# Two of four token groups turned by crossbar DMAs in the first phase of a gated attention and ReGLU training step

## The chip, the cores and the metric

The kernel runs on one core of one Trainium2 chip. The metric is the device time of one execution in microseconds (us); lower is better. The kernel before takes 909.8 us, the median of three runs (909.38 to 910.1).

## The reference

The program computes the output of a mixed layer and all its gradients for one sequence of 2048 tokens with 512 features, in bf16. For each token a gate g is the sigmoid of the product of x with a vector gate_w. One branch is a sliding-window attention with 32 heads of 16 features and a window of 256 tokens; the other is a feed-forward block with a ReLU gate and 1376 hidden columns. The part that matters for this change is the feed-forward block:

```
gate = x @ W_gate;  up = x @ W_up            # [2048,512] x [512,1376]
h    = relu(gate) * up
b    = h @ W_down
out  = g * attention(x) + (1 - g) * b
```

From grad_out the kernel also returns the gradients of x, wqkv, wo, W_gate, W_up, W_down and gate_w: eight outputs in all. For the feed-forward block, db = (1 - g) * grad_out, dh = db @ W_down^T, dg = dh * up where gate > 0, du = dh * relu(gate), and the weight gradients are x^T @ dg, x^T @ du and h^T @ db.

## The kernel before, in words

The program has three phases. The first, which the change is in, is the feed-forward block with its gradients (about the first quarter of the time). The second is the attention, forward and backward, and the third the output projections.

In the first phase the tokens lie in four groups of 512 (tg 0 to 3, TGW wide, each of four tiles of 128 tokens), and the hidden columns in 11 pieces of 128 (fc). One step is one piece for one group: 44 steps, the groups running fastest, so that steps 0 to 3 are fc 0 with the four groups, steps 4 to 7 are fc 1, and so on. The loop (L448) runs over n and does, in this order, for different steps at once:

- `gate` and `up` of step n (L365, L371): two products on TensorE (PE) of four matmuls each, from `x_T[tg]`, which holds the group's x with the features on the partitions. ScalarE (ACT) takes the ReLU into `rg`, VectorE (DVE) makes `upm`, and GpSimd (POOL) makes `hT`.
- `dh` of step n-2 (L379): a product of the turned W_down piece `WdT` with `db_T`, db with the features on the partitions; ACT copies it, DVE and POOL make dg and du, the two halves of the tile `dgu`.
- `turn_h` of step n-1 (L389) and `turn_dgu` of step n-4 (L393): crossbar DMAs on the queue of SyncE (SP), which turn `hT` and `dgu` into rows, `h_r` and `dgu_r`.
- `keep` (L398): plain DMAs on ACT's queue that store hT of step n-3 and dg and du of step n-4 to HBM.
- `weights` of step n-6 (L402): 20 matmuls on PE that add to the weight gradients, from the rows of x (`x_r`), `dgu_r`, `h_r` and the rows of db (`db_r`). So the first weights product, that of step 0, is in n = 6.

In the first steps there is more to do, once per group. `turn_x` (L292) turns a group's rows of x with 16 PE transposes of 128x128 into PSUM and two copies, one by DVE and one by ACT, into `x_T`; the x of group n+1 is turned in n. `gate_col` (L301) makes g of group n. `db_rows` (L312) scales the rows of grad_out into `db_r`: tiles 1 and 3 of the group on ACT, tile 0 on DVE, tile 2 on POOL (on DVE for the last group). `turn_db` (L321) turns them, again by 16 PE transposes and two copies, in step n+1 for group n.

The order of work is written out by hand: each engine runs its instructions in the order of the program. All loads and all crossbar DMAs stand on SP's queue, in the order of the program too. Ahead of the loop (L243 to L274) SP issues x of group 0, the first 128 columns of W_gate and W_up, x of group 1, grad_out of group 0, a piece of W_down, then x of group 2, grad_out of group 1, x of group 3, grad_out of group 2, columns 128 to 383 of both weights, grad_out of group 3, and last columns 384 to 1375 of both weights (992 KB each, `load_wgu(3 * P, F)`, L274). In the loop the queue takes `turn_h`, `turn_wd` (L227, W_down's next piece, at the first group of each fc), `turn_dgu` and, from n = 8, other turns and stores.

The tiles `dgu` have 6 buffers, `hT` 7; PSUM has 3 buffers for the products of the steps.

Of the kernel before, what the change touches and what calls it, by code (L numbers as in the profile page):

```python
# [22 lines left out]
def kernel(  # L23
# [20 lines left out]
    nc = tc.nc  # L44
    P = 128
    x_d = A_x[0]
# [4 lines left out]
    F = B_W_gate.shape[1]  # L51
# [7 lines left out]
    TGW = min(512, S)  # L59
    NTG = S // TGW  # L60
    TPG = TGW // P
# [5 lines left out]
    def evac(out, in_, eng=None):  # L67
        if eng is None:
            eng = ("act", "dve")[rr["i"] % 2]
            rr["i"] += 1  # L70
        if eng == "act":
            nc.scalar.copy(out, in_)  # L72
        elif eng == "dve":
            nc.vector.tensor_copy(out, in_)  # L74
        else:
            nc.gpsimd.tensor_copy(out, in_)
# [6 lines left out]
    dgT_d = dram.tile([F, S], BF, name="dgT_d")  # L83
    duT_d = dram.tile([F, S], BF, name="duT_d")
# [13 lines left out]
    def slot(tag):  # L98
        return big.tile([P, DC, TGW], BF, tag=tag, name=tag)

    x_T = [slot(f"x{tg}") for tg in range(NTG)]
# [96 lines left out]
    with ExitStack() as p1, tc.manual_schedule():  # L198
# [3 lines left out]
        db_r = ap1.tile([P, NT, D], BF, name="db_r")  # L202
        db_T = ap1.tile([P, DC, S], BF, name="db_T")
# [8 lines left out]
        def rows_of(ap, tg):  # L212
            return ap[tg * TGW:(tg + 1) * TGW, :].rearrange("(t p) d -> p t d", p=P)
# [6 lines left out]
        def load_go(tg):  # L220
            flat = zt[tg // 2][:].rearrange("p w k h q -> p (w k h q)")
            go_in[tg] = flat[:, (tg % 2) * TPG * D:(tg % 2 + 1) * TPG * D].rearrange("p (t d) -> p t d", t=TPG)
            nc.sync.dma_start(go_in[tg], rows_of(go_d, tg))
# [3 lines left out]
        def turn_wd(fc):  # L227
            WdT[fc] = fp.tile([P, DC, P], BF, tag="WdT", bufs=2, name="WdT")
            nc.sync.dma_start_transpose(out=WdT[fc][:], in_=B_W_down[start_of(fc):start_of(fc) + P, :])
# [3 lines left out]
        def turn_wd0():  # L233
            WdT[0] = fp.tile([P, DC, P], BF, tag="WdT", bufs=2, name="WdT")
            pt = ps1.tile([P, DC, 2, P], BF, tag="mm", bufs=3, name="ptw")
            for c in range(DC):
                nc.tensor.transpose(pt[:, c, 0, :], wd0[:, c * P:(c + 1) * P], ident[:])
            nc.vector.tensor_copy(WdT[0][:], pt[:, :, 0, :])
# [17 lines left out]
        def load_x(tg):  # L256
            nc.sync.dma_start(x_r[:, tg * TPG:(tg + 1) * TPG, :], rows_of(x_d, tg))

        def load_wgu(a, b):
            nc.sync.dma_start(Wg_sb[:, :, a:b], Wg_v[:, :, a:b])  # L260
            nc.sync.dma_start(Wu_sb[:, :, a:b], Wu_v[:, :, a:b])
# [3 lines left out]
        nc.sync.dma_start(Wu_sb[:, :, 0:W0], Wu_v[:, :, 0:W0])  # L265
        load_go(0)
        nc.sync.dma_start(wd0[:], B_W_down[0:P, :])
        load_x(2)
        load_go(1)
        load_x(3)  # L270
        load_go(2)
        load_wgu(W0, 3 * P)
        load_go(3)
        load_wgu(3 * P, F)  # L274
        nc.gpsimd.memset(par4[:], 1.0)
        nc.gpsimd.affine_select(out=par4[:], in_=par4[:], compare_op=ALU.is_ge, fill=0.0, base=0,
                                pattern=[[-32, P // 32]], channel_multiplier=1)
# [14 lines left out]
        def turn_x(tg):  # L292
            for half in range(2):
                t0 = tg * TPG + 2 * half
                pt = ps1.tile([P, DC, 2, P], BF, tag="tr", bufs=2, name="ptx")
                for c in range(DC):
                    for tt in range(2):
                        nc.tensor.transpose(pt[:, c, tt, :], x_r[:, t0 + tt, c * P:(c + 1) * P], ident[:])
                evac(x_T[tg][:, :, 2 * half * P:(2 * half + 2) * P], pt[:].rearrange("p c t q -> p c (t q)"), ("dve", "act")[half])

        def gate_col(tg):  # L301
            zps = ps1.tile([P, TPG], F32, tag="mm", bufs=3, name="zps")
            for k in range(TPG):
                t = tg * TPG + k
                for c in range(DC):
                    nc.tensor.matmul(zps[:, k:k + 1], lhsT=x_T[tg][:, c, k * P:(k + 1) * P], rhs=gw_col[:, c:c + 1],
                                     start=(c == 0), stop=(c == DC - 1))
            tsl = slice(tg * TPG, (tg + 1) * TPG)
            nc.scalar.activation(g_all[:, tsl], zps[:], ACT.Sigmoid)
            nc.vector.tensor_scalar(omg_all[:, tsl], g_all[:, tsl], -1.0, 1.0, op0=ALU.mult, op1=ALU.add)  # L310

        def db_rows(tg):  # L312
            for k in range(TPG):
                t = tg * TPG + k
                if k % 2:
                    nc.scalar.mul(db_r[:, t, :], go_in[tg][:, k, :], omg_all[:, t:t + 1])
                else:
                    eng = nc.gpsimd if k == 2 and tg < NTG - 1 else nc.vector
                    eng.tensor_scalar(db_r[:, t, :], go_in[tg][:, k, :], omg_all[:, t:t + 1], None, op0=ALU.mult)
# [45 lines left out]
        def gate(k):  # L365
            k.gps = ps1.tile([P, TGW], F32, tag="mm", bufs=3, name="gps")
            product(k.gps, lambda c: Wg_sb[:, c, k.fsl], lambda c: x_T[k.tg][:, c, :])
            k.rg = tile1("rg")
            nc.scalar.activation(k.rg[:], k.gps[:], ACT.Relu)  # L369
# [19 lines left out]
        def turn_h(k):  # L389
            k.h_r = fp.tile([P, TPG, P], BF, tag="h_r", bufs=6, name="h_r")  # L390
            nc.sync.dma_start_transpose(out=k.h_r[:], in_=k.hT[:])
# [6 lines left out]
        def keep(k, *pairs):  # L398
            for dst, src in pairs:
                nc.scalar.dma_start(dst[k.fsl, k.ts], src)  # L400
# [37 lines left out]
        def turn_gw():  # L438
            pt = ps1.tile([P, P], BF, tag="mm", bufs=3, name="ptg")
            nc.tensor.transpose(pt[:], gw_r[:], ident[:])  # L440
            nc.vector.tensor_copy(gw_col[:], pt[:, 0:DC])
# [6 lines left out]
        for n in range(N1 + 8):  # L448
            at = lambda lag: steps[n - lag] if 0 <= n - lag < N1 else None
            if at(0):  # L450
                gate(at(0))
                if 0 < n < NTG:
                    gate_col(n)
                if n == 2:
                    turn_wd0()
                if n + 1 < NTG:
                    turn_x(n + 1)
                if n == 0:
                    turn_gw()
                up(at(0))  # L460
                if n == 0:
                    gate_col(n)
                if n < NTG:
                    db_rows(n)
                if at(0).tg == 0 and at(0).fc > 0:
                    turn_wd(at(0).fc)
            if 1 <= n <= NTG:
                turn_db(n - 1)
            if at(2):
                dh(at(2))  # L470
            if at(1):
                turn_h(at(1))
            if at(3):
                keep(at(3), (hT_d, at(3).hT[:]))
            if at(4):
                turn_dgu(at(4))
                keep(at(4), (dgT_d, at(4).dgT), (duT_d, at(4).duT))
            if at(6):
                f = weights(at(6))
                if f is not None:  # L480
                    stores[n + 1] = f
            if n in stores:
                stores.pop(n)()
            t = n - DA0
            if t % 2 == 1 and 0 <= t // 2 < NT:
                make_da(t // 2)
            if t % 2 == 0 and 0 < t // 2 <= NT:
                turn_da(t // 2 - 1)
            if t == 2:
                nc.vector.reduce_sum(par[:, 0:1], par4[:], axis=AX.X)  # L490
                nc.vector.tensor_scalar(par[:, 1:2], par[:, 0:1], -1.0, 1.0, op0=ALU.mult, op1=ALU.add)
            if n == NTG + 1:
                nc.scalar.activation(tiny[:], tiny[:], ACT.Exp)
            if t in (NT + 3, 2 * NT + 1):
                i = (t - NT - 3) // (NT - 2)
                nc.gpsimd.memset(zt[i][:, 0, :, :, :], 0.0)
                nc.vector.memset(zt[i][:, 1, :, :, :], 0.0)
            if n == N1 - 2:
                first = project_parts(*groups[0])
            for _ in range({N1 + 1: 2, N1 + 2: 0}.get(n, 1)):  # L500
                if first:
                    first.pop(0)()
            if n == N1 + 2:
                second = project_parts(*groups[1])
            if n in (N1 + 2, N1 + 3, N1 + 4):
                second.pop(0)()
            z = n - DA0 - NT - 2
            if z == 0:
                load_w(0)
            if z % 4 == 3 and 0 < z // 4 + 1 < DC:  # L510
                load_w(z // 4 + 1)

    p3 = ctx
    if True:
# [333 lines left out]
        with tc.manual_schedule():  # L848
# [7 lines left out]
            n = 0  # L856
# [142 lines left out]
    with ExitStack() as p56:  # L999
        x_r5 = x_r  # L1000

        with ExitStack() as p6:
# [20 lines left out]
            for g in range(NG):  # L1023
# [3 lines left out]
                for tl in range(GT):  # L1027
                    t = g * GT + tl
# [108 lines left out]
```

## Time and profile before

| what | value |
| --- | --- |
| median of three runs | 909.8 us (909.38 to 910.1) |
| the profiled execution's own time | 911.05 us |
| its span, first to last instruction | 909.4 us |
| PE busy | 895.0 us (98%), 10711 matmuls |
| DVE, ACT, POOL busy | 511.8, 441.3, 491.7 us |
| DMA | 169.06 MB, 186 GB/s in the mean |
| SP's DMA queue (q1) | 145.51 MB, 86.8% of 16 engines |
| TensorE's granted clock | 1.0 |

A time in a view is in us from the first instruction of the span. PE is the matmul part of TensorE, PEld its weight loads; SPq, ACTq and so on are an engine's instruction queue, which issues DMAs. In a timeline a row gives the start, the length and what was done; in the chain of waits each row is a piece of the chain of work that ended last, so that a matmul is counted there by the distance to the next and not by its whole pipelined length. The landing of a DMA is the time from its issue to the semaphore that tells of its end.

### The profile page before, as it was taken

The numbers are of one execution on the slowest core, as the hardware profiler recorded it, in microseconds if no ns is written. First come the engines' busy times: TensorE is split into PE (matmuls) and PEld (weight loads), VectorE is DVE, ScalarE is ACT, GpSimd is POOL, SyncE is SP. The second block draws the span as 40 slices with busy tenths as digits, with TensorE's granted clock in tenths as the row PEclk, the third lists the DMA queues.
The fourth block names the chain that finished last, engine by engine and source line by source line (L and its number), as shares of the span: only waits on it lengthen the run. The fifth ranks groups of instructions, "written<-read, shape, count | busy, mean of one in ns | idle before, by whom it ended". The sixth has DMA issues, their size and how long they took to land.

```text
span 909.4 us, 26127 instructions
## 1 busy us (share of the span) xinstructions
PE 895.0 (98%) x10711; PEld 566.7 (62%) x10711; DVE 511.8 (56%) x952; ACT 441.3 (49%) x778; POOL 491.7 (54%) x937
## 2 busy tenths in 40 slices
PE   9999999999989999999999999999999999999998
PEld 5555656655657777667776677766777644444445
DVE  4433334324468887678886788876787222333223
ACT  6422232222278777667776677766788211100001
POOL 4644545545267778767777567875677312222221
PEclk9999999999999999999999999999999999999999
DMA  9998879999799999999999989999999998777731
GB/s 301 203 194 186 197 179 207 211 207 216 180 143 158 180 188 194 184 175 156 177 185 187 180 161 182 187 182 184 184 185 186 235 269 227 186 181 185 182 86 46
DMA packets 505575, 169.06 MB, mean 186 GB/s; under 512 B 433456, under 2 KB 504336, under 8 KB 505456
## 3 DMA queue, kind: packets, MB, share of 16 engines
q1 hardware_dynamic: 484816, 145.51, 86.8%
q10 hardware_dynamic: 19008, 17.31, 7.2%
q0 software_dynamic: 1632, 4.59, 1.4%
q8 instruction: 83, 1.36, 0.6%
q14 instruction: 36, 0.29, 0.1%
HBM read 32.28 MB, written 36.24 MB: 75 GB/s over the span
## 4 chain that ended last, share of the span: by engine, by line
PE 80%; DMA 5%; DVE 4%; POOL 3%; issue 3%; SPq 2%; ACT 2%; ACTq 0%; POOLq 0%; DVEq 0%
PE dxps L1062 8%; PE ST L683 8%; PE dPT L707 7%; PE pt L750 6%; PE wps L412 5%; PE wps L637 5%; PE dxps L1066 4%; PE CD L541 4%; PE bps L1035 4%; PE BA L721 4%; PE pp L133 4%; PE dps L414 3%; PE ups L363 3%; PE gps L363 2%; PE CD L544 2%
## 5 line engine op out<-in xcount | busy, mean ns | idle before, releaser
L683 PE MATMUL ST<-z,K 128*128 128x512 bf16 x360 | 135.8, 378 | 2.6 <-DVE PPm L712 1.2
L707 PE MATMUL dPT<-z,V 128*128 128x512 bf16 x360 | 136.0, 378 | 1.9 <-DVE Pd L712 0.5
L695 POOL TENSOR_SCALAR_AFFINE_SELECT PPd<-PPd 128x512 bf16<-128x512 bf16 x126 | 80.0, 635 | 86.7 <-ACT PPd L693 86.7
L377 POOL TENSOR_TENSOR hT<-rg,upm 128x512 bf16<-128x512 bf16 x44 | 51.8, 1176 | 116.0 <-DVE upm L375 104.3
L412 PE MATMUL wps<-dgu_r,x_r 128*128 128x256 bf16 (+1 forms) x704 | 103.9, 270 | 1.8 <-DVE wst L74 1.8
L712 DVE TENSOR_TENSOR PPd<-PPd,dPT 128x512 bf16<-128x512 bf16 x126 | 85.4, 678 | 18.3 <-PE dPT L707 9.1
L698 POOL TENSOR_SCALAR_AFFINE_SELECT Pu<-Pu 128x512 bf16<-128x512 bf16 x112 | 71.9, 642 | 31.8 <-ACT Pu L693 30.7
L412 PEld LDWEIGHTS <-x_r 128*128 128x128 bf16 x704 | 68.4, 98 | 33.1 <-issue 2.6
L712 DVE TENSOR_TENSOR Pd<-Pu,dPT 128x512 bf16<-128x512 bf16 x112 | 76.3, 681 | 21.5 <-POOL Pu L698 10.6
L693 ACT ACTIVATE PPd<-ST 128x512 bf16<-128x512 f32 x126 | 76.1, 605 | 22.0 <-PE ST L683 19.7
L712 DVE TENSOR_TENSOR PPm<-PPm,dPT 128x512 bf16<-128x512 bf16 x122 | 81.4, 668 | 7.8 <-PE dPT L707 6.1
L693 ACT ACTIVATE Pu<-ST 128x512 bf16<-128x512 f32 x112 | 67.4, 602 | 34.1 <-PE ST L683 33.6
L693 ACT ACTIVATE PPm<-ST 128x512 bf16<-128x512 f32 x122 | 73.7, 604 | 20.2 <-PE ST L683 19.6
L1042 ACT COPY a_sb<-aps 128x512 f32<-128x512 f32 x16 | 9.4, 586 | 151.4 <-issue 137.7
L375 DVE SCALAR_TENSOR_TENSOR upm<-rg,ups 128x512 bf16<-128x512 bf16 x44 | 30.1, 685 | 82.9 <-ACT rg L369 40.3
L369 ACT ACTIVATE rg<-gps 128x512 bf16<-128x512 f32 x44 | 26.3, 598 | 91.8 <-PE gps L363 44.2
L72 ACT COPY p<-pt 128x1024 bf16<-128x1024 bf16 x67 | 68.5, 1022 | 3.8
L414 PE MATMUL dps<-db_r,h_r 128*128 128x512 bf16 x176 | 66.7, 379 | 0.0
L387 POOL TENSOR_TENSOR dgu<-dh_sb,rg 128x512 bf16<-128x512 bf16 x44 | 56.7, 1289 | 5.3 <-ACT dh_sb L383 5.3
L1048 POOL DMA_DIRECT2D out_dram<-o_sb x16 | 8.7, 542 | 88.8 <-DVE o_sb L1046 82.4
L637 PE MATMUL wps<-rows_st,x_r 128*128 128x384 bf16 x256 | 50.3, 325 | 0.0
L133 PE MATMUL pp<-x,p 128*128 128x512 bf16 x192 | 49.0, 378 | 0.0
(193 smaller groups left out, 2357.5 us busy)
## 6 DMA issues: line engine op xcount, KB each, us to landing
dqkvo_d<-rows_st SPq DMA_DIRECT2D x15, 512.0 KB, 4.0
hT_d<-hT ACTq DMA_DIRECT2D x44, 128.0 KB, 2.5
dgT_d<-dgu ACTq DMA_DIRECT2D x44, 128.0 KB, 3.0
duT_d<-dgu ACTq DMA_DIRECT2D x44, 128.0 KB, 2.9
duT_g<-duT_d SPq DMA_DIRECT2D x8, 640.0 KB, 5.2
gt<-hT_d SPq DMA_DIRECT2D x7, 640.0 KB, 5.8
dgT_g<-dgT_d SPq DMA_DIRECT2D x7, 640.0 KB, 5.0
out_dram<-wst SPq DMA_DIRECT2D x20, 128.0 KB, 2.7
```

The lines of the kernel that those rows point to most:

```text
L72: nc.scalar.copy(out, in_)
L133: nc.tensor.matmul(pp[:], lhsT=w_p[c][:, cd, which * P:(which + 1) * P], rhs=x_T[tg][:, cd, :], start=(cd == 0), stop=(cd == DC - 1))
L412: nc.tensor.matmul(acc["w"][:, c, 0:2 * nw], lhsT=x_r[:, t, c * P:(c + 1) * P], rhs=k.dgu_r[:, :, i, s0:P], start=(go_ and c % 2 == 0), st ...
L414: nc.tensor.matmul(acc["d"][:], lhsT=k.h_r[:, i, :], rhs=db_r[:, t, :], start=go_, stop=no_)
L637: nc.tensor.matmul(wps[:], lhsT=x_r[:, t, part * P:(part + 1) * P], rhs=sts[c][:, t, 0:3, :], start=first and t == t0, stop=last and t == ...
L683: nc.tensor.matmul(ST[:], lhsT=KTt[:, ksl], rhs=z[:, 0, :, jl, :], start=True, stop=True)
L693: nc.scalar.activation(u.Pu[:], ST[:], ACT.Exp)
L695: nc.gpsimd.affine_select(out=u.Pu[:], in_=u.Pu[:], compare_op=ALU.is_ge, fill=0.0, base=0, pattern=[[0, HH], [1, P]], channel_multiplier=-1)
L698: nc.gpsimd.affine_select(out=u.Pu[:], in_=u.Pu[:], compare_op=ALU.is_ge, fill=0.0, base=-1, pattern=[[0, HH], [-1, P]], channel_multiplier=1)
L707: nc.tensor.matmul(u.dPT[:], lhsT=VTt[:, ksl], rhs=z[:, 1, :, jl, :], start=True, stop=True)
L712: nc.vector.tensor_tensor(out=u.Pd[:], in0=u.Pu[:], in1=u.dPT[:], op=ALU.mult)
L1062: nc.tensor.matmul(to, lhsT=src[:, fc, lsl], rhs=W6[(wt, fc)][:, cols], start=(fc == 0 and wt == "Wg"), stop=False)
```

## The change

For groups 2 and 3 the turns on PE go. `cross_x` turns x of a whole group by one crossbar DMA from HBM into `x_T[tg]`, and stands on SP's queue where `load_x(2)` and `load_x(3)` stood. `cross_db` turns each of a group's four tiles of db by one crossbar DMA from `db_r` into `db_T`, right behind `db_rows` of n = 2 and 3. The rows of x of these groups, still wanted by `weights`, are loaded in n = 3 and 4. The columns 384 to 1375 of W_gate and W_up are loaded in two parts, 384 to 895 in n = 5 and 896 to 1375 in n = 6. The stores of dg and du come a step later.

```
+        def cross_x(tg):
+            nc.sync.dma_start_transpose(out=x_T[tg][:], in_=x_d[tg * TGW:(tg + 1) * TGW, :])
+
+        def cross_db(tg):
+            for t in range(tg * TPG, (tg + 1) * TPG):
+                nc.sync.dma_start_transpose(out=db_T[:, :, t * P:(t + 1) * P], in_=db_r[:, t, :])
...
         nc.sync.dma_start(wd0[:], B_W_down[0:P, :])
-        load_x(2)
+        cross_x(2)
         load_go(1)
-        load_x(3)
+        cross_x(3)
         load_go(2)
         load_wgu(W0, 3 * P)
         load_go(3)
-        load_wgu(3 * P, F)
...
-                if n + 1 < NTG:
-                    turn_x(n + 1)
+                if n == 0:
+                    turn_x(1)
...
                 if n < NTG:
                     db_rows(n)
+                    if n >= 2:
+                        cross_db(n)
                 if at(0).tg == 0 and at(0).fc > 0:
                     turn_wd(at(0).fc)
-            if 1 <= n <= NTG:
+            if 1 <= n <= 2:
                 turn_db(n - 1)
...
             if at(4):
                 turn_dgu(at(4))
-                keep(at(4), (dgT_d, at(4).dgT), (duT_d, at(4).duT))
+            if at(5):
+                keep(at(5), (dgT_d, at(5).dgT), (duT_d, at(5).duT))
+            if n in (3, 4):
+                load_x(n - 1)
+            if n in (5, 6):
+                load_wgu(*((3 * P, 7 * P), (7 * P, F))[n - 5])
```

## The prediction

> **What bounds the kernel now.** I read the page's busy times first, then a table of engine busy time by stretch for the first phase, then the chain of waits there, then the timeline of SP's queue. The page says that PE is the bound nearly everywhere and that the DMA engines are close behind:
>
> ```profile
> PE 895.0 (98%) x10711; PEld 566.7 (62%) x10711; DVE 511.8 (56%) x952; ACT 441.3 (49%) x778; POOL 491.7 (54%) x937
> ...
> DMA  9998879999799999999999989999999998777731
> ```
>
> The change lies within the first 50 us. There the table by stretch (length, then busy time and instructions of PE, PEld, DVE, ACT, POOL, then granted clock, DMA share, GB/s) shows:
>
> ```profile
> 6.00:14.00 8.00, 7.65 (x97) 5.40 (x98) 4.31 (x9) 5.44 (x10) 2.74 (x2) 1.00 1.10 349
> 14.00:22.00 8.00, 8.00 (x108) 5.64 (x105) 4.69 (x12) 7.21 (x13) 5.95 (x5) 1.00 1.10 354
> 22.00:30.00 8.00, 7.58 (x56) 4.12 (x54) 5.34 (x8) 4.55 (x8) 5.41 (x5) 1.00 1.39 203
> 30.00:36.00 6.00, 5.59 (x34) 3.28 (x34) 1.32 (x3) 3.14 (x6) 2.38 (x2) 1.00 1.10 272
> 36.00:46.00 10.00, 10.00 (x64) 6.09 (x63) 3.99 (x6) 2.50 (x5) 7.11 (x6) 1.00 0.79 180
> ```
>
> PE is full from 14 us on, but for under a microsecond around 30 us; from 36 us it is full, at 5.20 us a step (gate at 35.72, 40.91, 46.11 in the timeline). So PE work that goes is worth its time, and each new PE stall before 36 us costs its time. The chain of waits around the one stall:
>
> ```profile
> 23.77 5.55 DMA WdT<-in_B_W_down_dram
> 29.32 0.02 issue
> 29.34 0.33 ACTq L400
> 29.66 0.04 issue
> 29.70 0.02 ACTq L369
> 29.72 0.04 issue
> 29.76 0.61 ACT rg L369
> 30.41 1.02 PE gps L363 x4
> ```
>
> A store on ACT's queue waited until a W_down turn, which it has nothing to do with, landed; the ReLU stood behind it, and PE lost 0.83 us. In the trace's DMA records SP's and ACT's DMAs take eight semaphores in turn (101 and 104 to 110), and each waits until the DMA before it on its semaphore has landed. That turn landed late because 2 MB of late weight columns lay ahead. Last, the two commonest crossbar DMAs of the phase, by line (ns: least, median, most; then a landing row each):
>
> ```profile
> L342 SPq DMA_TRANSPOSE d<-da_t x16: 1195/1231/1252, 56.2 to 215.2; - x16
> ...
> DMA to landing us min/median/max: 2.3/2.9/4.4
> ```
>
> ```profile
> L395 SPq DMA_TRANSPOSE dgu_r<-dgu x44: 1253/1300/2885, 27.6 to 242.5; - x44
> ...
> DMA to landing us min/median/max: 2.7/3.6/6.3
> ```
>
> SP is held about 1.2 us by each crossbar DMA, also where DMA is nearly idle. `turn_da` (L342) is the new `cross_db` in form: 128x512 from SBUF into a strided slice.
>
> **What goes.** Four sets of 16 PE transposes. A set is 0.89 us in the chain where it runs at pace (16.11): 4 x 0.89 = 3.6 us. Their eight copies (ACT 1.0, DVE 0.68 each, from the groups by line) go too, worth nothing: neither engine sets the pace. With the late weights out of the way the 0.83 us stall may go. If nothing were late, the gain would be 3.6 + 0.8 = 4.4 us. Played forward from gate 1 at 10.16 with 0.86 a product, 0.38 a gate column set, 0.25 W_down's turn and 0.89 a set, and one wait for POOL's `db_r` (13.55, as now), PE would be at gate 2 at 14.0, gate 3 at 18.1, gate 4 at 21.1, dh of step 2 at 22.8, and the first weights product at 28.8 instead of 33.0.
>
> **What cross_x adds.** Where 512 KB of rows took 512/349 = 1.5 us of DMA, the turn's 2048 packets of 256 B at 18 ns (DMA records) on 16 engines take 2.3, so 0.8 more. No row shows a 512 KB turn from HBM into x. The bounds: 0 more (rows' speed) and 2.9 more (half of the 8.8 us landing of the 1 MB `gt` turns is 4.4); I take 0.8, from the packets. x of group 2 landed at 4.91 + 6.75 = 11.66, so now near 12.5 to 14, and gate 2 wants it at 14.0: cover, just. grad_out of group 2 landed by 7.84 + 8.3 = 16.2; behind two turns it lands near 17.8 (16.2 to 22). SP's issue: the 512 KB `p2d` turns hold it 1.8 to 4.3, median 2.7; with five loads at 1.25 behind, SP is free at about 17, as now (16.1).
>
> **What cross_db adds.** No PE work, but eight crossbar DMAs in SP's order: turn_h 0; db tiles 8 to 11; turn_h 1; db 12 to 15; turn_h 2; x rows; turn_wd; turn_h 3; turn_dgu 0. Each waits for its `db_r`, and everything behind it waits too. db tile 8 needs grad_out at 17.8 and a scaling of 0.7: 18.6. From there one start every 1.28 us (57.52 after 56.22, 58.77 after 57.52):
>
> - db 11 starts 18.6 + 3 x 1.28 = 22.4 and lands 2.9 later at 25.3. dh of step 2 wanted it at 22.8: stall 2.5.
> - db 15 starts 18.6 + 8 x 1.28 = 28.8, lands 31.7. PE is ready at 25.3 + 3 x 0.86 = 27.9: stall 3.8.
> - turn_wd starts near 32.0 (turn_h 2, then 0.6 for x rows) and lands 4 later (least 3.4, median 5.0) at 36.0. PE is ready at 34.3: stall 1.7.
> - turn_dgu 0 starts 18.6 + 11 x 1.28 + 1.35 + 0.6 = 34.6 and lands 3.2 to 3.3 later (2.7 to 3.6) at 37.9. PE is ready at 36.9: stall 1.0.
>
> The first weights product is at 37.9 instead of 33.0: **4.9 us later**. This is the whole sum: 9.0 of stalls, less 4.2 gained up to there. ACT's stores, each tied to a DMA eight back, hold the ReLU in these stalls too, mostly inside them.
>
> **What is only moved.** From there PE again needs 5.2 a step. turn_dgu 1 starts near 37.5, lands at 41; wanted at 42.6. The late weights are issued in n = 5 and 6, some 0.6 to 1.4 us of SP each; 1 MB takes 3 us of DMA, so turn_dgu 2 lands at 46 to 48; wanted at 48.3. That cover is thin: nothing to 1.5 us, I take nothing. Columns 384 on are wanted in n = 12, near 66: covered. x rows of groups 2 and 3 are wanted in n = 8 and 9: covered. Storing dg and du a step later removes two tied stores from n = 4; the six `dgu` buffers are freed at k + 5 and reused at k + 8, so it costs nothing and its worth lies inside the stalls.
>
> Sum: the profiled 911.05 (span 909.4) becomes about 916.0; on the median of the runs, 1.25 lower, 909.8 + 4.9 = 914.7.
>
> **Rivals.**
>
> *The turns are hidden and PE work is what counts: 909.8 - 4.4 = 905.4.* For it: plain loads were issued 0.5 us apart at the start, so SP can be quick. It needs the first weights product no later than 28.8. It is not slower than before from a spacing of (33.0 - 3.3 - 18.6 - 0.6) / 12 = 0.87 us downward. Against it: 1.19 is the least of the 60 turns above, and 1.20 the median of the 44 `h_r` turns. On the page "DMA: Bandwidth & Descriptors", section "Issuing engines are not separate DMA queues", the Trainium skill calls the sequencer's time to start a DMA usually small beside the DMA itself. By that rule this rival would win; the rows disagree, 1.2 of 2.9 us. Chance 0.14.
>
> *The stalls are long enough to slow TensorE's clock: 917.* The L254 matmuls ahead of 6 us take 627 ns, against 378 later, at the same size; the profile grants full clock from there on, and its longest later PE stall, 1.6 us, left it so. A 3.8 us stall is outside what this trace shows. At the start the clock was granted 5.3 us after the first matmul (1.27 to 6.6); half speed for as long loses 2.6, of which the stalls behind hide some: 916 to 917.3. The Trainium skill's page "TensorE: Matmul & The Clock Gate" (Part 1) gives about 3.4 us of idle as the point where the clock halves; so it speaks against the change, at the edge; no run here shows it yet. Chance 0.10.
>
> *The data are early: within 0.2%.* grad_out of group 2 at 16.2, tile 8 at 16.9, landings at their least (2.7 for `dgu`): the weights start at 35.5, 2.5 late, and the later waits around 200 us (1.6 us before a weights product) take part of it back: 910 to 912. Chance 0.12.
>
> *The forecast*, 914.7, including thin covers that break (to 918): 0.64.
>
> That the turns don't replace the PE work I leave out: the diff removes the calls.
>
> **Numbers.** A run of this kernel can tell 0.2%, 1.8 us, from no change. Faster 0.14, same 0.12, slower 0.74 (0.64 + 0.10). The range, 910.0 to 919.5, holds the forecast, the slowed clock and most of the early data; below it lies the hidden-turns rival, above it grad_out at 22 (4 us more).
>
> **What would show it.** In SP's timeline eight turns of `db_T` with starts 1.2 to 1.35 apart between 18 and 30 us; PE idle before dh of steps 2 and 3, released by DMAs into `db_T`, in all 8 to 10 us before 40; first weights product near 38; PE full after. Wrong: those starts under 0.9 apart; gate 2 waiting past 15 for x; PE idle again at steps 8 to 12 for `dgu_r`; or the loss there and a gain later, around 200 us, where ACT's stores are tied to other DMAs.

## The result, and the profile after

The median of five runs is 918.44 us (916.42 to 919.13), beside 909.8 (908.91 to 910.88) for the kernel before on the same chip: a ratio of 1.0088, with an interval of 1.0077 to 1.0100. The change costs 8.6 us of median. The forecast was 914.7, in a range up to 919.5, so the sign and the range hold, and the size is 3.7 us short.

The profiled execution of the kernel after took 916.42 us (span 914.7), 5.4 more than the profiled one of before. It is the fastest of its five runs, and the one of before lay 1.25 us above its median. So where the two traces are compared step by step, they show less than the medians do.

The page of the kernel after, busy times and DMA row:

```profile
PE 888.9 (97%) x10547; PEld 563.8 (62%) x10647; DVE 511.0 (56%) x948; ACT 438.2 (48%) x774; POOL 493.8 (54%) x937
...
DMA  9898778999979999999999989999999999778731
```

PE has 64 matmuls less to do (by its weight loads, 10647 for 10711), and the kernel is longer. The busy times, 888.9 and 895.0 us, don't size what went: the profile of after lacks 100 matmul records (10547 beside 10647 weight loads). The table by stretch of the kernel after, over the stretches shown of before (length, busy time and instructions of PE, PEld, DVE, ACT, POOL, then granted clock, DMA share, GB/s):

```profile
6.00:14.00 8.00, 7.25 (x72) 4.77 (x73) 3.32 (x6) 3.64 (x7) 1.31 (x2) 0.79 1.03 252
14.00:22.00 8.00, 6.85 (x85) 4.59 (x85) 4.73 (x9) 5.82 (x12) 6.53 (x5) 1.00 1.07 270
22.00:30.00 8.00, 6.13 (x27) 2.56 (x27) 5.69 (x8) 4.34 (x9) 5.97 (x6) 1.00 0.72 147
30.00:36.00 6.00, 2.15 (x8) 0.82 (x8) 0.98 (x2) 0.60 (x2) 2.01 (x3) 0.92 0.47 93
36.00:46.00 10.00, 8.41 (x41) 4.11 (x41) 1.61 (x4) 3.15 (x5) 3.52 (x3) 0.88 1.13 261
```

From 30 to 36 us little is busy: PE 2.15 of 6 us, and the DMA engines move 93 GB/s where they moved 272. A stretch in which all engines and the transfers are mostly idle suggests a chain of small things that wait for each other. The chain of waits of the kernel after names them:

```profile
24.84 2.46 DMA db_T<-db_r
27.30 0.14 issue
27.43 1.02 PE dhps L369 x4
...
31.42 2.52 DMA db_T<-db_r
33.94 0.09 issue
34.03 1.04 PE dhps L369 x4
...
37.23 3.69 DMA dgu_r<-dgu
40.95 0.60 PE wps L418 x4
```

The last db turn of group 2, the last of group 3, then `turn_dgu` 0, and the first weights product at 40.95 instead of 33.0: 7.95 us later (the forecast said 4.9). PE's stalls there, from the gaps in its timeline, are 1.46 and 3.85 us (dh of steps 2 and 3, for db), 1.33 (dh of step 4, for the next W_down piece) and 0.21 (the weights, for `dgu_r`). The eight turns themselves, by line:

```profile
L264 SPq DMA_TRANSPOSE db_T<-db_r x8: 1191/1216/1252, 20.9 to 31.4; - x8
...
DMA to landing us min/median/max: 2.4/2.5/3.3
```

And SP's queue, in its timeline (start, length, what):

```profile
4.92 5.38 SPq L260 DMA_TRANSPOSE x<-in_A_x_dram  x1
...
10.99 3.58 SPq L260 DMA_TRANSPOSE x<-in_A_x_dram  x1
14.61 0.58 SPq L223 DMA_DIRECT2D z<-in_grad_out_dram  x1
...
20.94 5.12 SPq L264 DMA_TRANSPOSE db_T<-db_r  x4
26.11 1.26 SPq L397 DMA_TRANSPOSE h_r<-hT  x1
27.46 5.18 SPq L264 DMA_TRANSPOSE db_T<-db_r  x4
...
34.61 1.19 SPq L229 DMA_TRANSPOSE WdT<-in_B_W_down_dram  x1
...
37.23 1.36 SPq L401 DMA_TRANSPOSE dgu_r<-dgu  x1
```

The two x turns hold SP 4.4 and 2.9 times as long as the median db turn does (1.22 us). The kernel before already has such a hold, on a 128 KB turn from SBUF with the 2 MB of late weight columns ahead of it:

```profile
18.87 3.44 SPq L391 DMA_TRANSPOSE h_r<-hT  x1
```

The turn ahead of it, at 16.17, took 2.60 us. POOL had written the `hT` of these two by 15.65 and 11.96, so they did not wait for their data.

From 20.94 to 42 us SP is never idle for more than 0.1 us: what stands behind a turn starts when the turn lets SP go. Gate starts are late by 1.88 us at step 1, 0.74 at step 4, 7.84 at step 7, and from step 8 to step 30 by the same 7.93. So the loss is made before 44 us and only carried after it. Then 0.13 comes back at step 31 and 1.71 at step 39, where the profiled execution of before waited 1.55 us near 200 us. Of the other kernels' profiles only that of experiment 8 has a wait of that size at this step (1.42 us at 208 us); that of 10 has 1.92 us at 186 us. I read this return as belonging to that one execution of before, and 7.9 as near to what the medians show; with one profiled execution of before this is not shown.

### The profile page after: what moved, and what is told of

Same layout as the page of the kernel before. It is cut to its first block, busy times and chain, and to the rows that moved or that the text cites. A ratio compares the mean times of both kernels' runs of the same rounds, so it can differ in the third digit from the quotient of the medians.

```text
span 914.7 us, 25900 instructions
## 1 busy us (share of the span) xinstructions
PE 888.9 (97%) x10547; PEld 563.8 (62%) x10647; DVE 511.0 (56%) x948; ACT 438.2 (48%) x774; POOL 493.8 (54%) x937
## 3 DMA queue, kind: packets, MB, share of 16 engines
HBM read 32.28 MB, written 36.24 MB: 75 GB/s over the span
## 4 chain that ended last, share of the span: by engine, by line
PE 83%; DVE 5%; ACT 3%; POOL 3%; DMA 2%; issue 2%; SPq 1%; ACTq 0%; DVEq 0%; POOLq 0%
PE wps L418 9%; PE dxps L1075 8%; PE ST L696 7%; PE dPT L720 7%; PE pt L763 5%; PE wps L650 5%; PE dxps L1079 4%; PE dhps L369 4%; PE bps L1048 4%; PE CD L554 4%; PE dps L420 4%; PE BA L734 4%; PE gps L369 4%; PE pp L133 3%; PE ups L369 3%; PE CD L557 2%
## 5 line engine op out<-in xcount | busy, mean ns | idle before, releaser
L706 ACT ACTIVATE PPd<-ST 128x512 bf16<-128x512 f32 x126 | 76.1, 605 | 22.1 <-PE ST L696 18.6
L420 PE MATMUL dps<-db_r,h_r 128*128 128x512 bf16 x158 | 59.9, 379 | 0.0
L369 PE MATMUL dhps<-db_T,WdT 128*128 128x512 bf16 x175 | 44.9, 379 | 6.8 <-DMA db_T<-db_r 5.3
L392 DVE TENSOR_TENSOR dgu<-dh_sb,upm 128x512 bf16<-128x512 bf16 x44 | 32.3, 735 | 33.4 <-ACT dh_sb L389 30.5
```

Source lines behind the costliest of these rows:

```text
L369: nc.tensor.matmul(out[:], lhsT=w(c), rhs=x(c), start=(c == 0), stop=(c == DC - 1))
L420: nc.tensor.matmul(acc["d"][:], lhsT=k.h_r[:, i, :], rhs=db_r[:, t, :], start=go_, stop=no_)
L706: nc.scalar.activation(u.Pu[:], ST[:], ACT.Exp)
```

## The experiments

Ratios are to the kernel before on the same chip, with a 95% interval; "weights" is the start of the first weights product in the profiled execution (33.0 before, 40.95 after).

**1. The db of groups 2 and 3 back on PE** (the x turns stay):

```
-                    if n >= 2:
-                        cross_db(n)
...
-            if 1 <= n <= 2:
+            if 1 <= n <= NTG:
                 turn_db(n - 1)
```

> The changed kernel with db of all groups turned on PE again; x of groups 2 and 3 is still turned by crossbar DMAs, late weights and stores as changed. Queue theory (SP's eight db turns at 1.28 us each delay the first weights product): that product comes near 32 to 34 us instead of 41.0, and the time falls to 905 to 909. Rival (the x turns, which held SP for 5.4 and 3.6 us at the start, cost most): the time stays at 913 or more.

912.75 us, 1.0029 (1.0019 to 1.0039); weights at 33.67. The queue's part came as expected, the time did not: something else costs 2.6 us. The waits of this kernel between 14 and 22 us (engine, line, what it waited for: total, times, longest):

```profile
ACT db_r L322 <- DMA z<-in_grad_out_dram: 3.6, 2, 1.9
...
PE ups L369 <- ACT rg L375: 1.5, 1, 1.5
```

The x turns hold SP for 5.45 and 3.48 us, grad_out of group 1 behind the first lands at 14.79, ACT's scaling waits for it, the ReLU behind that is late, and PE finds no free PSUM buffer.

**2. The x of groups 2 and 3 back on PE** (the db turns stay):

```
-        cross_x(2)
+        load_x(2)
         load_go(1)
-        cross_x(3)
+        load_x(3)
...
-                if n == 0:
-                    turn_x(1)
+                if n + 1 < NTG:
+                    turn_x(n + 1)
...
-            if n in (3, 4):
-                load_x(n - 1)
```

> The changed kernel with x of groups 2 and 3 loaded as rows at the start and turned on PE again; db of these groups is still turned by eight crossbar DMAs, late weights and stores as changed. Queue theory: the first db turn starts near 18 to 19 instead of 20.9, the first weights product near 38 to 39, so 914 to 917. Rival (x turns cost most): under 910.

919.2 us, 1.0097 (1.0084 to 1.0110); weights at 40.87, `turn_dgu` 0 issued at 37.39, stalls of 1.28 and 3.63 for db. With the x turns gone the whole loss is there: the db turns carry it, and this is a miss for the smaller loss I expected (914 to 917). It doesn't size the x turns: in this profile TensorE had its full clock only from 10.69 us, which made PE itself late at the start, and the first db turn still started at 20.68.

**3. One db turn a group instead of four** (the same bytes in 512 KB turns; `db_T` laid out by tile):

```
-            for t in range(tg * TPG, (tg + 1) * TPG):
-                nc.sync.dma_start_transpose(out=db_T[:, :, t * P:(t + 1) * P], in_=db_r[:, t, :])
+            ts = slice(tg * TPG, (tg + 1) * TPG)
+            nc.sync.dma_start_transpose(out=db_T[:, ts, :, :].rearrange("p t c q -> p (t c) q"),
+                                        in_=db_r[:, ts, :].rearrange("p t d -> p (t d)"))
```

> The changed kernel with one crossbar DMA for each group's db (512 KB) in place of four of 128 KB; same bytes, db_T laid out by token tile. Queue theory (number of issues on SP counts): two issues of 1.3 to 2.7 us in place of eight of 1.28, turn_dgu 0 starts near 32 instead of 37.2, first weights product near 36, time 911 to 915. Rival (the crossbar's own speed and landing count, not the issue): dh of steps 2 and 3 wait as long or longer, 917 to 920.

915.46 us, 1.0063 (1.0051 to 1.0075), just above the queue theory's 911 to 915, and weights at 36.60, as it has them. SP's timeline of this kernel:

```profile
21.89 1.95 SPq L264 DMA_TRANSPOSE db_T<-db_r  x1
...
25.67 1.88 SPq L264 DMA_TRANSPOSE db_T<-db_r  x1
...
32.56 1.39 SPq L402 DMA_TRANSPOSE dgu_r<-dgu  x1
```

Two turns hold SP for 3.8 us where eight held it for 10.3. `turn_dgu` 0 starts 10.7 us after the first db turn instead of 16.3; the first one itself comes 0.95 us later, since it waits for all four tiles. The bytes are the same: what fell is the number of issues. In this profile the clock was half from 36.5 to 39.9 us, over the first weights product, which took 4.20 us instead of 2.61; so some 1.6 us of what is left of the loss is the clock's.

**4, 6 and 7. The other two edits on the kernel before**: both, the stores alone, the weight columns alone.

```
-        load_wgu(3 * P, F)
...
+            if n in (5, 6):
+                load_wgu(*((3 * P, 7 * P), (7 * P, F))[n - 5])
```

```
-                keep(at(4), (dgT_d, at(4).dgT), (duT_d, at(4).duT))
+            if at(5):
+                keep(at(5), (dgT_d, at(5).dgT), (duT_d, at(5).duT))
```

> The kernel before with only the late weight columns loaded in steps 5 and 6 and dg and du stored a step later; all turns on PE as before. Queue theory: the 0.83 us stall near 30 us goes, 908 to 909.5. Rival (tied stores: the 1.6 us stall near 200 us went in the changed kernel because the stores moved): 907 to 908, with no stall near 200.

> The kernel before with only dg and du stored a step later. Queue theory: within 0.5 us of before, the 0.83 us stall near 30 us shrinks or stays. Rival (tied stores): the 1.6 us stall near 200 us goes and the time falls to 908 to 909.3.

> The kernel before with only the late weight columns loaded in two parts in steps 5 and 6. Queue theory: the stall near 30 us goes, 909 to 910. Rival (more DMAs on the queue in steps 5 and 6 make the first dgu turns late): 910.5 to 912.

Both: 909.87 us, 0.9990 (0.9981 to 0.9999). The stores alone: 908.8, 0.9987 (0.9978 to 0.9996). The columns alone: 910.41, 1.0001 (0.9992 to 1.0009). The stall of 0.83 us near 30 us is gone from all three profiles, so either edit alone removes it; for the stores alone the queue theory had it shrink or stay. The wait near 200 us is gone from all three as well, also where the stores stayed, so the moved stores don't account for it. The times don't choose between the theories: 909.87 and 910.41 lie outside both ranges given for them, and 908.8 lies in the rival's, 908 to 909.3. None of the changes is as much as 0.2%; the stores a step later have the lowest median of the study, with an interval that overlaps that of both. So the whole loss is the turns'.

**5. Experiment 1 with the grad_out loads ahead of the x turns**:

```
-        cross_x(2)
         load_go(1)
-        cross_x(3)
+        cross_x(2)
         load_go(2)
+        cross_x(3)
```

> Crossbar turns for x of groups 2 and 3 only (db on PE, late weights and stores as changed), but grad_out of group 1 is issued ahead of the x turn of group 2, and grad_out of group 2 ahead of the x turn of group 3. Theory from the trace of the kernel with db on PE: its loss of about 2 us comes from the x turn holding SP for 5.4 us, so that grad_out of group 1 lands at 14.8 instead of 13.2, ACT's scaling and the ReLU behind it are late and PE waits 1.5 and 0.7 us for PSUM. Then here grad_out of group 1 lands by 12.5, the waits of 1.5 go, and the time is 907 to 910. Rival (the x turns land too late for the gates): 911 to 914.

910.46 us, 1.0000 (0.9992 to 1.0009), above the expected 907 to 910 and below the rival's 911. grad_out of group 1 lands at 11.18 instead of 14.79, the wait of 1.48 us is gone, and weights start at 31.46. The intervals of 1 and 5 lie apart, so the loss of experiment 1 is the place of the grad_out loads behind turns that hold SP. But with two sets of turns (1.8 us) off PE and the weights 1.5 us earlier, there is no gain in the time. In the profile a wait of 1.41 us at 237 us, which that of before doesn't have, takes about as much back; whether every run has it isn't known.

**8. Eight small turns that nothing waits for.** In the kernel of experiment 4, where all turns are on PE, SP issues eight crossbar DMAs of 128x128 (32 KB) from `db_r` into a tile that is never read, at the places of the db turns:

```
+        aside = ap1.tile([P, 2 * TPG, P], BF, name="aside")
...
+        def small_db(tg):
+            for t in range(tg * TPG, (tg + 1) * TPG):
+                nc.sync.dma_start_transpose(out=aside[:, t - 2 * TPG:t - 2 * TPG + 1, :], in_=db_r[:, t, 0:P])
...
+                    if n >= 2:
+                        small_db(n)
```

> All turns on PE, late weights and stores as changed, and eight added crossbar DMAs of 128x128 (32 KB, a quarter of a db turn) from db_r into a tile that nothing reads, where the changed kernel has its db turns. What is added serves nothing but the test. Queue theory (each crossbar DMA holds SP 1.2 us whatever its size): starts 1.2 to 1.3 apart, turn_dgu 0 starts near 35 to 37, first weights product 38 to 40, time 913 to 916. Rival (bytes count): issues of 0.3 to 0.6 us, time within 1.5 of the same kernel without them (909.9).

918.54 us, 1.0092 (1.0078 to 1.0105), and weights at 38.36. By line:

```profile
L262 SPq DMA_TRANSPOSE aside<-db_r x8: 1130/1182/1760, 19.5 to 30.3; - x8
...
  ACT rg L373: 3.0, 1
...
DMA to landing us min/median/max: 2.2/2.3/3.8
```

A quarter of the bytes, nearly the same hold on SP (1.18 for 1.22 us), and the loss of the whole change although PE turns everything itself and its clock is full from 5.3 us on. The second line is under "who waited for it": a ReLU on ACT. ACT's queue held a store of hT until the h turn issued at 25.14 had landed; the store went out at 27.60, then the ReLU ran, and PE lost 1.11 us before the gate of step 5. The next store was held until the last small turn, issued at 30.33, had landed at 32.61; that is the 3.0 us of the second line, and PE lost 2.27 before the gate of step 6. After that it lost 0.45 for W_down, 1.28 for the first `dgu_r` and 1.45 behind it, and further steps some more. The time is above the 913 to 916 that I expected; I had not counted the ACT waits. So db's lateness and the bytes are not needed for this loss; the eight issues are enough, by SP's order and through the semaphores by which ACT's stores wait for SP's DMAs. How much is each, this run doesn't part.

**9. The h turns of steps 1 to 3 behind `turn_dgu` 0**:

```
-            if at(1):
+            if at(1) and not 2 <= n <= 4:
                 turn_h(at(1))
...
+                if n == 4:
+                    for k in steps[1:4]:
+                        turn_h(k)
```

> The changed kernel with one thing moved in SP's queue: the h turns of steps 1, 2 and 3 stand behind turn_dgu 0 in n = 4 instead of between the db turns and ahead of turn_dgu 0. Same work. Queue theory: turn_dgu 0 starts 3 x 1.28 = 3.8 us earlier, first weights product at 37 to 38 instead of 41.0, time 914 to 916. Rival (landing of the db turns or the slowed clock sets the end): 917 to 920.

919.23 us, 1.0096 (1.0081 to 1.0112). Weights at 38.24, close to the expected 37 to 38; the time was a miss, within the rival's 917 to 920. PE's timeline of this kernel (in brackets, the idle time before and what ended it):

```profile
42.58 1.03 PE L369 MATMUL dhps<-db_T,WdT 128*128 128x512 bf16 x4
47.45 0.60 PE L418 MATMUL wps<-dgu_r,x_r 128*128 128x256 bf16 x4 [3.85 <-DMA dgu_r<-dgu]
47.89 0.57 PE L420 MATMUL dps<-db_r,h_r 128*128 128x512 bf16 x1
```

The wait moved to the second weights product: `turn_dgu` 1 was now issued at 41.73. And the last line shows a second price, a matmul of 0.57 us where the others of its form take 0.38: after 3.85 us without work the granted clock is 0.5 for 3.41 us (47.95 to 51.36), and step 7 to step 8 took 10.88 = 5.20 + 3.85 + 1.83.

**10. Two db turns, h turns behind, loads first, all together**; **11. The loads first, alone**, in the kernel after (the edit of 5).

> The changed kernel with a short queue: one db DMA for each group (512 KB), the h turns of steps 1 to 3 behind turn_dgu 0, and grad_out of groups 1 and 2 issued ahead of the x turns. All PE turns of groups 2 and 3 stay away as in the change. Queue theory: first weights product near 32 (31 to 34), time 908 to 911. Rival (crossbar turns are too slow whatever the queue): 913 or more.

> The changed kernel with only grad_out of groups 1 and 2 issued ahead of the x turns; eight db turns stay. Queue theory: the first db turn starts near 19 instead of 20.9, first weights product near 39, time 916 to 917.5. Rival (the x turns' place costs nothing): 918 to 919.

10: 916.47 us, 1.0067 (1.0054 to 1.0080), a miss, on the rival's side (913 or more). The db turns wait for POOL's tile of group 2 until 22.6, weights are at 35.91 (not the 32 I expected), and stalls of 2.65 and 2.81 us are left. 11: 917.69, 1.0079 (1.0067 to 1.0092), inconclusive beside the 1.0088 of after. In its profile the x turns hold SP for 6.58 and 6.18 us, and grad_out of group 2 still lands at 19.29. The first db turn starts at 22.17, not near 19, and weights are at 42.74, not near 39: both expectations missed. So the advantage that the same edit had in experiment 5 doesn't show beside the db turns.

**12. Only group 3 by db turns**:

```
-                    if n >= 2:
+                    if n >= 3:
                         cross_db(n)
...
-            if 1 <= n <= 2:
+            if 1 <= n <= 3:
                 turn_db(n - 1)
```

> The changed kernel with db of group 2 turned on PE again and only the four db turns of group 3 left on SP's queue. Queue theory, now with what the h turns behind showed (all of SP's work up to turn_dgu 1 counts, whatever its order): four starts of 1.28 less, so about half way between the kernel with no db turns (1.0029 of before) and the changed one (1.0088): ratio 1.005 to 1.007, first weights product at 36 to 38. Rival (the loss comes with the first db turns, those of group 2, since dh waits for them): 1.002 to 1.004.

918.56 us, 1.0093 (1.0076 to 1.0110): both expectations missed. Four turns cost what eight cost. SP's timeline:

```profile
18.56 2.66 SPq L397 DMA_TRANSPOSE h_r<-hT  x2
25.17 5.12 SPq L264 DMA_TRANSPOSE db_T<-db_r  x4
...
32.28 2.55 SPq L229 DMA_TRANSPOSE WdT<-in_B_W_down_dram  x1
```

SP stood idle from 21.2 to 25.17, with the first of them at its head, until grad_out of group 3 had landed (23.82) and its first tile was scaled; then the four held it 5.1 us, the W_down turn went out at 32.28, PE waited 3.84 us for it, and `turn_dgu` 0 went out at 36.19, weights at 40.45. The clock was half from 37.6 to 44.4, and this weights product took 4.55 us instead of 2.62. So the price isn't the number of turns times 1.28. A turn that waits for its data at the head of the queue holds the queue for as long. I read this off the trace afterwards; no run tests it by itself.

## Why the prediction was right or wrong

- **What bounds the kernel there**: right. Not PE but what PE waits for, in the first 44 us, and 5.2 us a step after it.
- **The spacing of the db turns**: right. Starts 1.28 to 1.34 apart (forecast 1.28). From the first to `turn_dgu` 0 it took 16.29 us, forecast 11 x 1.28 + 1.95 = 16.03.
- **What cross_x adds**: the step that failed in size. The transfer was cheap: x of group 2 landed at 12.41 (forecast 12.5 to 14). But the turns held SP for 5.38 and 3.58 us; I took 2.7, the median of `p2d` turns that ran later, and the first of the two lies above the range I had quoted with it (1.8 to 4.3). SP was free at 18.1, not 17, grad_out of group 2 landed at 19.51, not 17.8, and DVE scaled tile 8 in 1.31 us, not 0.7. The first db turn started at 20.94 instead of 18.6, 2.3 us late. Add 0.3 in the queue and 0.4 in the landing of `dgu` (3.7 for 3.3): 3.0 of the 3.05 us that are missing at the first weights product. So the forecast's line that SP is held about 1.2 us by each crossbar DMA fails for those at the start, as the rows of 2.60 and 3.44 us in the kernel before show, and a median from later in the program was the wrong row to take.
- **The gain against it**: 4.2 us up to there, forecast, and none of it came. The forecast has PE 2.2 us ahead of before at gate 4; it was 0.74 behind. The loads behind the x turns, and a start at half clock (7.7 to 11.1 us), held it up. So the sum was right in form, stalls less gain, with 6.85 less -1.1 for 9.0 less 4.2; the stalls were smaller than forecast because PE itself came late.
- **What is only moved**: right. The late weights and the stores change less than 0.2% (experiments 6 and 7); from step 8 to step 30 not one wait is added, so the thin cover of the `dgu` turns held. (By the forecast's own 5.2 us a step, `turn_dgu` 1 was wanted at 37.9 + 5.2 = 43.1, not 42.6; nothing hangs on it.)
- **The hidden turns**: fell. Starts 1.28 apart, not under 0.87, and experiment 8 shows SP held for as long by 32 KB. The rule that I weighed there, from the Trainium skill's page "DMA: Bandwidth & Descriptors" ("Issuing engines are not separate DMA queues"), that starting a DMA takes little beside the DMA, doesn't hold for these: 1.18 us of 2.3 in experiment 8.
- **The slowed clock**: it happened, and did not set the time. After the stall of 3.85 us the clock was half from 35.0 to 38.4, but PE had little to do there and waited for W_down until 39.7. Experiment 8 has the same loss at full clock. In experiments 3, 9 and 12 the half clock fell on work and cost 1.6, 1.8 and 1.9 us, so this rival's price is real where PE has work when the clock is half.
- **The data early**: fell. grad_out came at 19.5, past the middle of the bounds (16.2 to 22).
- **Left open**: the profiled execution of after, late by 7.9 at step 30, is the fastest of its five; what the others lose beyond it isn't seen. Their mean granted clock is 0.994 to 0.998, that of the runs of before 0.998 to 1.0. The waits of about a microsecond near 200 us, which differ from kernel to kernel, were not tested by themselves. That ACT's tied stores take a part is shown in experiment 8, its size isn't. No run issues the turns from another engine's queue.

## What to carry to other kernels

Work that moves from a busy engine to a DMA queue is not free of time: here it was paid in the order of the queue that issues it. So count issues and the waits at the queue's head before bytes, and follow what stands behind. Where PE, the other engines and the DMA engines are mostly idle together, look at a queue's order. If such turns are wanted, make few of them (experiment 3) and put the loads that others wait for ahead of them, which helped with the x turns alone (experiment 5) and not visibly beside the db turns (experiment 11). Here even the best form, experiment 5, only came back to the time before.

## What the hardware showed that was not expected

- **Up to 256 KB a crossbar DMA holds the issuing queue by the issue, hardly by size**: in the median 1.18 us for 32 KB (experiment 8), 1.22 for 128 KB (`db_T`, after), 1.30 for 256 KB (`dgu_r`, before). At 512 KB from SBUF it took 1.9 in experiment 3, and 1.8 to 4.3 for the `p2d` turns of before.
- **At the start, with loads under way, it can hold far longer**: 3.5 to 6.6 us for 512 KB from HBM, where a plain load of 512 KB in the same place took 0.48 (before) or 0.74 (experiment 8), and 2.60 and 3.44 us for 128 KB from SBUF in the kernel before. How much of it is the source, the size or the loads was not taken apart.
- **The clock halves on idle time in sum, not on one long wait.** In all profiles the granted clock changes on a grid of 3.41 us. On that grid, in the first 260 us and past the first window at full clock, every full-clock window in which PE was without a matmul for 2.18 us or more in sum was followed by one at half, in seven cases: 2.18 (experiment 3), 2.43 (after), 2.55 (11), 2.63 (2), 2.65 (10), 2.92 (9) and 3.20 (12). None with 1.92 or less was. In experiment 3 the 2.18 us were made of two waits, one of 1.06 and one of 1.25 of which 1.12 fell in the window. In the first window at full clock less was enough: 1.81 us (after) and 1.93 (10); 1.72 (experiment 8) was not. The Trainium skill's page "TensorE: Matmul & The Clock Gate" (Part 1, and "HAM oscillation") has the window of 3.4 us, and the trace agrees with its length; it gives a gap of over about 3.4 us as the condition, and these runs show less to be enough.
